# Column sums of exp(phi): four fp32 adds on GpSimd and two fp32 matmuls in place of eighteen bf16 matmuls

## Chip, cores and metric

One core of one Trainium2 chip. The metric is the device time of one execution in microseconds (us). The kernel before takes 271.17 us (median of three runs, 270.51 to 271.28). Engines are named as in the profile: PE is TensorE, PEld its weight loads, DVE VectorE, ACT ScalarE, POOL GpSimd, SP SyncE. "L207" is line 207 of the kernel in question; the changed kernel's lines are shifted by up to twelve.

## The reference

Attention through 32 memory slots, then a two-layer network with a residual, for 8 batches of 8 heads, 576 positions and head size 64:

```python
a = np.exp(phi - np.max(phi, axis=2, keepdims=True))
a = a / (np.sum(a, axis=2, keepdims=True) + 1e-09)     # sum over the 576 positions
k_m = np.einsum('bhsm,bhsd->bhmd', a, k)
v_m = np.einsum('bhsm,bhsd->bhmd', a, v)
scores = scale * np.matmul(q, k_m.transpose(0, 1, 3, 2))
# ... softmax over the 32 slots, times v_m, heads side by side: x (8, 576, 512)
xn = (x - mu) / np.sqrt(var + 1e-06) * g_ln
out = x + np.maximum(xn @ w_ch1, 0.0) @ w_ch2
```

The change concerns only the sum over positions in the second line.

## The kernel before

The maximum is left out. A position is (partition, slot): 64 partitions by nine slots for each half of the heads. The sum over positions is a matmul with a column of one constant (`ones8`, which holds 8.0 and is called a column of ones below), for each slot and half, accumulated in PSUM: eighteen small matmuls in each batch, behind the 72 that make k_m and v_m.

```python
def a_exp(b):
    phi_st, kv, q_bf = loaded[b]
    e = att.tile([P, NS, 4, M], BF16, name="e_sb")
    nc.scalar.activation(out=e..., in_=phi_st..., func=AF.Exp)          # L195

def a_kv(b):
    kv_ps = big([P, 2, 512], FP32, "kv_ps")
    # ... 72 matmuls with e as weights and k|v as moving data: L207
    for c in range(NS):
        for g in range(2):
            r = TS * g
            nc.tensor.matmul(kv_ps[:, g, P:P + 1],                       # L214
                             e[r:r + TS, c].rearrange("p j m -> p (j m)"), ones8[r:r + TS, :],
                             start=(c == 0), stop=(c == NS - 1), tile_position=(r, 0))
    # ... k2 (ACT; in batch 0 DVE) and v2 (DVE) copied out of kv_ps
    nc.vector.reciprocal(out=rs, in_=kv_ps[:, :, P])
```

`a_tr` then transposes k2 and v2 on PE, `a_sc` computes the scores; its exponential uses `rs`. In the steady loop, batch b+1 is prepared between groups of eight matmuls of the second product of batch b:

```python
for b in range(1, B):
    mm1(b, 0, JC)                       # first product, 64 matmuls
    # after group 0 of the second product: a_exp(b+1), a_qT(b+1), a_kv(b+1)
    # after group 1: a_tr(b+1), x_tiles(...)
    # ... a_w1b, a_sc, a_den; at the end load(b+2)
```

Pool issues the loads of k, v and q and, in the start-up, casts three quarters of the second weight to bf16. A copy of one element holds the loads of that weight back until a part of the first has arrived:

```python
def w2_load(n, queue):
    st = wst.tile([P, 4, C], FP32, name="w2_st", bufs=3)
    if n == 0:
        nc.gpsimd.tensor_copy(out=st[0:1, 0, 0:1], in_=w1r[0:1, 3, 1024:1025])   # L143
    queue.dma_start(out=st, in_=w2_v[:, 4 * n:4 * (n + 1), :])
def w2_cast(n):
    nc.gpsimd.tensor_copy(out=w2b[:, 4 * n:4 * (n + 1), :], in_=w2_st[n])        # L148
# ...
w2_load(0, nc.sync)
w2_load(2, nc.sync)
# ...
warm(24)            # matmuls on constants
a_exp(0)
```

## Time and profile before

| | before |
|---|---|
| median time | 271.17 us |
| span of the profiled run | 270.6 us |
| PE busy | 243.6 us, 90% |
| POOL busy | 29.7 us, 11% |
| first transposes (batch 0) | 17.91 us |
| first transposes of batch 1 | 51.32 us |
| matmuls of k and v start, batches 2 to 7 | 76.71, 107.63, 134.30, 165.22, 191.89, 222.82 us |

A line of the timeline gives start, duration, engine, line, operation, output and inputs, sizes and a count; brackets tell how long the engine had been idle before it and what ended that. The granted clock is TensorE's clock in a stretch, as a share of full speed. From 76.71 us on the kernel repeats itself (30.92 and 26.67 us in turn).

### The profile page before, as it was taken

The numbers are of one execution on the slowest core, as the hardware profiler recorded it, in microseconds if no ns is written. First come the engines' busy times: TensorE is split into PE (matmuls) and PEld (weight loads), VectorE is DVE, ScalarE is ACT, GpSimd is POOL, SyncE is SP. The second block draws the span as 40 slices with busy tenths as digits, with TensorE's granted clock in tenths as the row PEclk, the third lists the DMA queues.
The fourth block names the chain that finished last, engine by engine and source line by source line (L and its number), as shares of the span: only waits on it lengthen the run. The fifth ranks groups of instructions, "written<-read, shape, count | busy, mean of one in ns | idle before, by whom it ended". The sixth has DMA issues, their size and how long they took to land.

```text
span 270.6 us, 5662 instructions
## 1 busy us (share of the span) xinstructions
PE 243.6 (90%) x2392; PEld 136.2 (50%) x2423; DVE 153.6 (57%) x302; ACT 128.1 (47%) x218; POOL 29.7 (11%) x47
## 2 busy tenths in 40 slices
PE   6487995985999999999999999999999999999992
PEld 4343562332754366446644475447543665466440
DVE  2227562448638664678375943886386646784431
ACT  3156654051754547255727174448545372555210
POOL 8210053700030000300030003000000000000000
PEclk9968999899999999999999999999999999999998
DMA  6999999999949449792889184965422491121133
GB/s 192 228 207 208 317 311 219 182 208 224 274 76 219 109 86 197 119 221 64 202 135 209 40 209 73 218 147 129 99 49 45 90 198 41 41 55 24 42 76 78
DMA packets 45058, 39.63 MB, mean 146 GB/s; under 512 B 19940, under 2 KB 38376, under 8 KB 45032
## 3 DMA queue, kind: packets, MB, share of 16 engines
q0 software_dynamic: 14784, 16.19, 36.2%
q1 hardware_dynamic: 29192, 21.44, 33.6%
q10 hardware_dynamic: 1056, 1.64, 1.6%
q8 instruction: 19, 0.31, 0.5%
q14 instruction: 7, 0.06, 0.1%
HBM read 41.42 MB, written 9.44 MB: 188 GB/s over the span
## 4 chain that ended last, share of the span: by engine, by line
PE 72%; DMA 12%; DVE 7%; ACT 5%; issue 2%; POOL 0%; DVEq 0%; POOLq 0%
PE ch_ps L396 40%; PE h_ps L338 20%; DMA phi_st<-in_phi_dram 7%; DMA kv_bf<-in_v_dram 5%; PE o_ps L366 3%; PE kv_ps L207 3%; DVE Eh L302 2%; PE w1b_ps L317 2%; ACT rden L299 2%; DVE w1b L321 1%; DVE bst L374 1%; PE sc_ps L280 1%; ACT rden L301 1%; ACT x_sb L370 1%; DVE x_sb L400 1%
## 5 line engine op out<-in xcount | busy, mean ns | idle before, releaser
L396 PE MATMUL ch_ps<-w2b,rT 128*128 128x512 bf16 x547 | 129.5, 382 | 6.2 <-DVE x_sb L400 3.1
L396 PEld LDWEIGHTS <-rT 128*128 128x128 bf16 x576 | 54.4, 98 | 66.3 <-issue 11.4
L338 PE MATMUL h_ps<-Eh,w1b 128*128 128x288 bf16 x512 | 66.7, 285 | 2.8 <-DVE Eh L302 1.6
L344 ACT ACTIVATE rT<-h_ps 128x576 bf16<-128x576 f32 x88 | 52.2, 649 | 29.9 <-PE h_ps L338 29.9
L338 PEld LDWEIGHTS <-w1b 128*128 128x128 bf16 x512 | 49.6, 97 | 19.7 <-issue 4.6
L346 DVE TENSOR_SCALAR rT<-h_ps 128x576 bf16<-128x576 f32 x40 | 30.3, 756 | 27.1 <-PE h_ps L338 27.1
L321 DVE SCALAR_TENSOR_TENSOR w1b<-m_sb,rsum,w1b_ps 128x512 bf16<-128x512 f32 x64 | 43.6, 739 | 2.4 <-ACT m_sb L181 2.0
L370 ACT ACTIVATE x_sb<-o_ps 128x1024 f32<-128x1024 f32 (+1 forms) x20 | 18.8, 938 | 38.9 <-PE o_ps L366 38.9
L400 DVE SCALAR_TENSOR_TENSOR x_sb<-ch_ps,rstd,x_sb 128x512 f32<-128x512 f32 x36 | 26.7, 743 | 16.1 <-PE ch_ps L396 16.1
L374 DVE BATCH_NORM_STATS2 bst<-x_sb 128x6 f32<-128x512 f32 x36 | 24.4, 678 | 13.3 <-ACT x_sb L370 13.3
L302 DVE SCALAR_TENSOR_TENSOR Eh<-E_sb,rs,rden 128x576 bf16<-128x576 bf16 x16 | 12.4, 814 | 17.1 <-ACT rden L301 17.1
L285 ACT ACTIVATE E_sb<-sc_ps,rs 128x640 bf16<-128x640 f32 x16 | 11.9, 791 | 15.7 <-PE sc_ps L280 15.6
L83 POOL DMA_DIRECT2D kv_bf<-in_k_dram x8 | 6.2, 771 | 107.4 <-PE kv_ps L214 106.3
L382 ACT ACTIVATE rstd<-mv,eps_sb 128x2 f32<-128x2 f32 (+1 forms) x20 | 5.9, 295 | 17.0 <-DVE mv L375 17.0
L366 PE MATMUL o_ps<-vb,Eh 128*128 128x256 bf16 (+1 forms) x80 | 12.0, 276 | 1.0 <-DVE Eh L302 1.0
L195 ACT ACTIVATE e_sb<-phi_st 128x1152 bf16<-128x1152 f32 x8 | 9.2, 1151 | 7.4 <-DMA phi_st<-in_phi_dram 7.4
L317 PE MATMUL w1b_ps<-w1r,kvT 64*32 64x512 bf16 x256 | 11.4, 390 | 1.1 <-DVE kvT L238 0.6
L299 ACT ACTIVATE rden<-den_ps 128x576 f32<-128x576 f32 x16 | 9.5, 644 | 5.0 <-PE den_ps L297 5.0
L186 PE MATMUL w_ps<-vmask,blk 128*128 128x256 bf16 x58 | 8.7, 313 | 2.4 <-DVE vmask L130 2.4
L225 DVE CAST v<-kv_ps 128x128 bf16<-128x128 f32 x8 | 2.3, 286 | 15.1 <-ACT k L223 15.1
L207 PE MATMUL kv_ps<-kv_bf,e_sb 64*32 64x128 bf16 x576 | 6.8, 232 | 4.0 <-ACT e_sb L195 3.0
L301 ACT ACTIVATE rden<-rden 128x576 f32<-128x576 f32 x16 | 10.0, 683 | 0.0
(58 smaller groups left out, 116.5 us busy)
## 6 DMA issues: line engine op xcount, KB each, us to landing
out_dram<-x_sb SPq DMA_DIRECT2D x72, 128.0 KB, 2.4
kv_bf<-in_k_dram POOLq DMA_DIRECT2D x8, 576.0 KB, 6.6
kv_bf<-in_v_dram POOLq DMA_DIRECT2D x8, 576.0 KB, 9.7
phi_st<-in_phi_dram SPq DMA_DIRECT2D x7, 576.0 KB, 4.6
q_bf<-in_q_dram POOLq DMA_DIRECT2D x7, 576.0 KB, 12.0
w1r<-in_moe_w_ch_dram POOLq DMA_DIRECT2D x4, 512.0 KB, 17.4
w_st<-in_moe_w_ch_dram SPq DMA_DIRECT2D x2, 1024.0 KB, 16.3
q_st<-in_q_dram SPq DMA_DIRECT2D x1, 1152.0 KB, 11.1
```

The source lines that it names most:

```text
L207: nc.tensor.matmul(kv_ps[32 * j:32 * (j + 1), g, 0:P], e[r:r + TS, c, j, :], kv[r:r + TS, j, :, D * c:D * (c + 1)], start=(c == 0), stop=( ...
L302: nc.vector.scalar_tensor_tensor(out=Eh[:, g, :], in0=s["E"][:, g, 0:S], scalar=s["rs"][:, g:g + 1], in1=rd[:, g].rearrange("p a x -> p (a ...
L317: nc.tensor.matmul(ps[32 * j:32 * (j + 1), g, :], s["kvT"][r:r + 64, 2, 32 * j:32 * (j + 1)], w1r[r:r + 64, j, fs], start=True, stop=True, ...
L321: nc.vector.scalar_tensor_tensor(out=s["w1b"][:, g, fs], in0=m_sb[:, fs], scalar=s["rsum"][:, g:g + 1], in1=ps[:, g, :], op0=ALU.mult, op1 ...
L338: nc.tensor.matmul(h_ps[:, half, 0:HS], s["w1b"][:, g, P * j:P * (j + 1)], s["Eh"][:, g, HS * half:HS * (half + 1)], start=(g == 0), stop= ...
L344: nc.scalar.activation(out=dst, in_=h_ps[:, :, 0:HS], func=AF.Relu)
L346: nc.vector.tensor_scalar(out=dst, in0=h_ps[:, :, 0:HS], scalar1=0.0, scalar2=None, op0=ALU.max)
L366: nc.tensor.matmul(ov[:, :, g, :], s["Eh"][:, g, a:z], s["vb"][:, g].rearrange("p j d -> p (j d)"), start=True, stop=True)
L370: nc.scalar.activation(out=x[:, 0:n], in_=o_ps[:, 0:n], func=AF.Copy)
L374: nc.vector.bn_stats(out=stt, in_=x[:, i, :])
L396: nc.tensor.matmul(ch_ps, rT[:, j, P * t:P * (t + 1)], w2b[:, j, :], start=(j == 0), stop=(j == JC - 1))
L400: nc.vector.scalar_tensor_tensor(out=x, in0=ch_ps, scalar=rstd, in1=x, op0=ALU.mult, op1=ALU.add)
```

## The change

The intent is to take work off PE, the busiest engine, and give it to Pool, the idlest: Pool adds the nine slots in fp32 (slots 0 to 3 to slots 4 to 7, then two of the four results to the other two, then one to one, then the ninth slot), and PE sums over partitions with one fp32 matmul for each half. These two stand ahead of the transposes.

```diff
-    ones8 = consts.tile([P, 1], BF16, name="ones8")
+    ones8 = consts.tile([P, 1], FP32, name="ones8")
@@ a_exp
+        es = att.tile([P, P], FP32, name="es")
+        ev = e.rearrange("p c j m -> p c (j m)")
+        nc.gpsimd.tensor_tensor(out=a4, in0=ev[:, 0:4], in1=ev[:, 4:8], op=ALU.add)     # L200
+        nc.gpsimd.tensor_tensor(out=a2, in0=a4[:, 0:2], in1=a4[:, 2:4], op=ALU.add)     # L202
+        nc.gpsimd.tensor_tensor(out=es, in0=a2[:, 0], in1=a2[:, 1], op=ALU.add)         # L203
+        nc.gpsimd.tensor_tensor(out=es, in0=es, in1=ev[:, 8], op=ALU.add)               # L204
@@ a_kv
-        for c in range(NS):
-            for g in range(2):
-                ... the eighteen matmuls, L214 above
@@ new
+    def a_sum(b):
+        for g in range(2):
+            r = TS * g
+            nc.tensor.matmul(kv_ps[:, g, P:P + 1], s["es"][r:r + TS, :], ones8[r:r + TS, :],
+                             start=True, stop=True, tile_position=(r, 0))               # L235
+        nc.vector.reciprocal(out=rs, in_=kv_ps[:, :, P])
@@ a_tr
+        a_sum(b)
         t_ps = big([P, 3, P], BF16, "kvT_ps")
```

## The prediction

> **What bounds the kernel now.** I read the page first: engine shares and the chain that ended last.
>
> ```profile
> span 270.6 us, 5662 instructions
> ## 1 busy us (share of the span) xinstructions
> PE 243.6 (90%) x2392; PEld 136.2 (50%) x2423; DVE 153.6 (57%) x302; ACT 128.1 (47%) x218; POOL 29.7 (11%) x47
> ...
> PE 72%; DMA 12%; DVE 7%; ACT 5%; issue 2%; POOL 0%; DVEq 0%; POOLq 0%
> ```
>
> TensorE (PE) is the bound on average, and Pool looks free. But the chain is 12% DMA, so the kernel has two stages. I split the span with the table by stretch (columns: length, busy time of PE, PEld, DVE, ACT and POOL, granted clock, DMA share, GB/s):
>
> ```profile
> 13.65:17.90 4.25, 3.30 (x112) 2.46 (x112) 0.47 (x2) 2.70 (x3) 1.14 (x2) 0.70 1.24 207
> 17.90:21.35 3.45, 3.23 (x33) 1.05 (x33) 0.91 (x5) 1.48 (x2) 0.00 (x0) 0.50 1.24 206
> ...
> 42.30:45.27 2.97, 0.01 (x1) 0.00 (x0) 0.00 (x0) 1.21 (x2) 1.38 (x1) 1.00 1.13 207
> 45.27:51.50 6.23, 6.01 (x108) 3.10 (x109) 1.89 (x6) 2.13 (x6) 4.53 (x8) 0.73 1.23 164
> ...
> 165.20:191.90 26.70, 26.25 (x283) 14.82 (x287) 17.73 (x34) 14.69 (x25) 2.48 (x4) 1.00 0.76 155
> 191.90:222.80 30.90, 29.95 (x295) 16.71 (x299) 19.45 (x37) 15.67 (x28) 0.00 (x0) 1.00 0.42 84
> ```
>
> From 76.7 us on, one batch takes 26.7 or 30.9 us and PE is busy for 97 to 98% of it: what PE executes or waits for there is paid for in full. The first 45 us are different: PE has holes, one of 2.97 us at 42.30 because phi of batch 1 lands late. The clock was low around 18 us and again after that hole (0.73).
>
> The concerned stretch of a steady batch, from the timeline (start, duration, engine, line, operation; batch 6 is prepared here):
>
> ```profile
> 190.69 1.15 ACT L195 ACTIVATE e_sb<-phi_st 128x1152 bf16<-128x1152 f32 x1
> 191.89 0.80 PE L207 MATMUL kv_ps<-kv_bf,e_sb 64*32 64x128 bf16 x72
> 192.63 0.38 PE L214 MATMUL kv_ps<-ones,e_sb 64*128 64x1 bf16 x18
> 193.16 1.67 PE L396 MATMUL ch_ps<-w2b,rT 128*128 128x512 bf16 x7 [0.16 <-issue]
> 194.67 0.27 PE L234 MATMUL kvT_ps<-ident,k 128*128 128x128 bf16 x2
> ```
>
> The eighteen sum matmuls hold PE from 192.69 to 193.00, 0.31 us in the chain of waits (0.31 to 0.33 in every batch): 17 ns each, though each record says 160 ns, because they are pipelined. Then come eight matmuls of the second product and the transposes at 194.67, that is 2.83 us after the exponential ended (191.84).
>
> **What the Trainium skill says.** "GPSIMD Engine Reference", section 3.1: a two-input fp32 add takes about 2.6 cycles per element, 4497 ns for 2048 elements. The trace has no Pool add; its one-input casts of 2048 elements take 1895 ns, a copy of one element 0.18 us. "FP8 and Floating Point Precision", TensorE Precision Notes: true fp32 takes four passes through the array. "TensorE: Matmul & The Clock Gate", weight-path section: the fast weight load is not used for fp32, and loading takes the columns over 1.2 (128 columns: 107 ns). The trace has no fp32 matmul, so it neither confirms nor denies these two. The same page, Part 1: after an idle window of about 3.4 us the clock halves, and it returns after a busy window. The trace agrees: PE idles 3.67 us before 13.65, and the granted clock is then 0.70 and 0.50.
>
> **The change part by part, steady batches.** (a) Removed: eighteen matmuls, 0.31 us of PE per batch. (b) Added on PE: two fp32 matmuls with 128 columns of weights each. My estimate from the skill: four loads of 107 ns make 0.43 us for one matmul; the two use different row halves and may overlap in part, or not at all: 0.25 to 0.9, taken as 0.5 us. So the replacement of eighteen by two saves nothing. (c) Added on Pool: adds of 512, 256, 128 and 128 elements, in series, 1024 in all. At 4497/2048 = 2.2 ns an element that is 2.25 us, plus a start and a handover for each of four dependent instructions; with the 0.1 to 0.2 us that small Pool instructions take here, 2.6 to 3.2 us (estimate). (d) Moved: the sums now stand just ahead of the transposes in PE's order, and PE takes instructions in order. Without the eighteen, PE gets there at 194.67 - 0.31 = 194.36, which is 2.5 us after the exponential. The Pool sums are ready 2.6 to 3.2 us after it, plus 0.1 to 0.2 for the two semaphores: PE waits 0.2 to 0.9, I take 0.5. Sum per batch: -0.31 + 0.5 + 0.5 = +0.7 us. Six batches (2 to 7) are prepared in the steady stage: 6 x 0.7 = +4.2 us. The reciprocal moves behind the sums but its user, the score exponential at 199.89, is 5 us away; it costs nothing.
>
> **The prologue.** This is the larger term. The built order of Pool shows where the adds of batch 0 fall: not right after the exponential (done at 5.9 us) but after the one-element copy of line 143, which holds back the loads of the second weight until a piece of the first one has landed. Pool's timeline, PE's timeline and the chain of waits of the kernel before:
>
> ```profile
> 23.50 0.17 POOL L143 CAST w_st<-w1r 1x1 f32<-1x1 bf16 x1 [6.62 <-DMA w1r<-in_moe_w_ch_dram]
> ...
> 17.91 0.39 PE L234 MATMUL kvT_ps<-ident,k 128*128 128x128 bf16 x2
> ...
> 38.70 3.61 PE L396 MATMUL ch_ps<-w2b,rT 128*128 128x512 bf16 x15
> 45.27 0.80 PE L207 MATMUL kv_ps<-kv_bf,e_sb 64*32 64x128 bf16 x72 [2.96 <-ACT e_sb L195]
> ...
> 24.19 19.85 DMA phi_st<-in_phi_dram
> ```
>
> Pool cannot begin the adds of batch 0 before 23.7; they end at 26.3 to 26.9. PE, which went to the transposes at 17.91, now waits some 9 us for the sums, and with two cold fp32 matmuls reaches them at about 27.1: **9.2 us late**. All of the first batch (scores, exponentials, the first product) follows from there, in order, up to the end of the first quarter of the second product (42.3 before). PE is cold after this wait, as it was before, but some 1.5 us more of the work falls into the cold time: +0.6. So that quarter ends near 42.3 + 9.2 + 0.6 = 52.1. Before, PE then waited until 45.27 for phi of batch 1. That load is issued by ScalarE after the logarithms of batch 0, so it too goes 9.2 us later (33.4); but the same bytes are in flight before and after at over 200 GB/s, and all of them had landed by 47.2 before, so I expect it by 48, while ScalarE gets to this exponential at about 48.6. So the hole of 2.97 us goes. The low clock after it goes too: the next sixteen matmuls took 5.07 us (46.41 to 51.48) and should take some 3.6 at full clock. The transposes of batch 1 are then at 52.1 + 0.8 + 3.6 + 0.4 = 56.9 against 51.5: **+5.4 us** remain of the 9.2, and nothing later has slack to take them up.
>
> Sum: 271.2 + 5.4 + 4.2 = 280.8; I say 280.5.
>
> **Loads.** Pool also issues the k, v and q loads. Before, those of batch b+2 are issued as soon as the matmuls of batch b free the buffer (77.83, 108.75 in the trace); now they stand behind the adds of batch b+1, a whole batch later (near 110 for the one of 77.83). They are needed one batch (27 to 31 us) after that and take 6.6 to 12 us to land: no wait.
>
> **The rivals.** R1, no wait in steady batches: Pool adds at the one-input rate (0.93 ns an element) would end 1.5 us after the exponential, and with cheap fp32 matmuls (0.25 us) the steady batches change by nothing: 276.5. For it: the skill's add figure is for fp32 inputs, half of these are bf16. Against it: two operands share one read port there. R2, Pool much slower (mixed types, dependent handovers; 4.5 us for the chain): a wait of 2 us per batch, 6 x 2.2 = 13 and the prologue +7: 291. R3, the prologue wait is hidden, because the stage is bound by transfers: then +1 to +4 in all, 272 to 275. Against it: only 2.97 us of hole plus the clock loss stand between the prologue's PE chain and its end, less than 9. R4, what the change intends: eighteen matmuls of 160 ns each off PE, 8 x 2.9 = 23 us saved. Against it: the chain shows 0.31 us, not 2.9; even with free sums the most is 8 x 0.31 = 2.5 us, under 1%.
>
> **Range and chances.** The prologue term is 4 to 8, the steady term -1 to +9; both positive in most draws: 276 to 287 holds it 8 times in 10. Faster by 2% would need all of R3 and more: 0.01. Within 2% (below 276.6): R1 or R3, 0.13. Slower: 0.86.
>
> **What would show it right or wrong.** In the profile of the changed kernel: a PE hole of 8 to 9 us from about 18 to 26.5, ended by Pool's last add, with the copy of line 143 just before the adds; no hole before the matmuls of batch 1, which start near 52; Pool's four adds about 1.2, 0.65, 0.35 and 0.35 us apart; six PE waits of 0.2 to 0.9 us on Pool; two fp32 matmuls costing 0.25 to 0.9 us before the transposes; batches of 27.4 and 31.6 us; no wait for k, v or q loads. I am wrong if the adds of batch 0 run early, if phi of batch 1 lands after 50, or if the Pool chain differs from 2.6 to 3.2 us.

## The result, and the profile after

The changed kernel takes **284.5 us** (median of four runs, 284.3 to 285.44), against 271.23 us (median of four runs, the three above and one more) before. The ratio is 1.0497, with a 95% interval of 1.0462 to 1.0532: slower by 5%. Ratios here are the mean time of one kernel's fast runs over that of the other's of the same rounds, so not quite the ratio of the medians.

The shares of the chain that ended last, by engine, of the kernel after:

```profile
PE 62%; ACT 11%; DVE 9%; POOL 8%; DMA 6%; issue 2%; POOLq 0%; DVEq 0%
```

Pool was 0% of this chain and is now 8%. One steady batch of the kernel after, from the timeline:

```profile
174.20 1.15 ACT L195 ACTIVATE e_sb<-phi_st 128x1152 bf16<-128x1152 f32 x1
175.40 0.80 PE L215 MATMUL kv_ps<-kv_bf,e_sb 64*32 64x128 bf16 x72
175.43 1.15 POOL L200 TENSOR_TENSOR es<-e_sb 128x512 f32<-128x512 bf16 x1 [25.94 <-ACT e_sb L195]
176.65 0.72 POOL L202 TENSOR_TENSOR es<-es 128x256 f32<-128x256 f32 x1
177.45 0.45 POOL L203 TENSOR_TENSOR es<-es 128x128 f32<-128x128 f32 x1
177.98 0.42 POOL L204 TENSOR_TENSOR es<-es,e_sb 128x128 f32<-128x128 f32 x1
178.46 0.39 PE L235 MATMUL kv_ps<-ones,es 64*128 64x1 f32 x4 [0.43 <-POOL es L204]
178.78 0.29 PE L246 MATMUL kvT_ps<-ident,k 128*128 128x128 bf16 x2
```

From the first matmul of k and v to the transposes it was 194.67 - 191.89 = 2.78 us, and is 178.78 - 175.40 = 3.38. The difference of 0.60 is paid in each steady batch: the starts of these matmuls are now 85.05, 116.58, 143.86, 175.40, 202.67 and 234.20, so five batches take 149.15 us in place of 146.11.

The start-up of the kernel after, Pool and PE, from the timeline:

```profile
22.99 0.17 POOL L143 CAST w_st<-w1r 1x1 f32<-1x1 bf16 x1 [6.64 <-DMA w1r<-in_moe_w_ch_dram]
23.14 1.14 POOL L200 TENSOR_TENSOR es<-e_sb 128x512 f32<-128x512 bf16 x1
...
26.17 0.59 PE L235 MATMUL kv_ps<-ones,es 64*128 64x1 f32 x4 [9.09 <-POOL es L204]
26.69 0.39 PE L246 MATMUL kvT_ps<-ident,k 128*128 128x128 bf16 x2
...
55.05 0.80 PE L215 MATMUL kv_ps<-kv_bf,e_sb 64*32 64x128 bf16 x72
```

PE waits 9.09 us for the adds of batch 0, whose input had been ready since 5.8 us. The wait for phi of batch 1 that stood in this place before (2.96 us, ahead of the matmuls at 45.27) is gone: at 55.05 no wait is shown. But the whole start-up is later than I had predicted (55.05 and not 52.1), and between the transposes and those matmuls stands something that the prediction does not have. DVE, Pool and PE in the same stretch:

```profile
32.88 3.18 DVE L314 SCALAR_TENSOR_TENSOR Eh<-E_sb,rs,rden 128x576 bf16<-128x576 bf16 x2 [0.50 <-ACT rden L313]
33.03 2.41 POOL L148 CAST w2b<-w_st 128x2048 bf16<-128x2048 f32 x1 [6.92 <-DMA w_st<-in_moe_w_ch_dram]
37.25 1.86 PE L350 MATMUL h_ps<-Eh,w1b 128*128 128x288 bf16 x8 [0.25 <-ACT rT L356]
...
44.35 3.73 POOL L148 CAST w2b<-w_st 128x2048 bf16<-128x2048 f32 x2 [8.91 <-DMA w_st<-in_moe_w_ch_dram]
...
46.54 1.88 DVE L262 TENSOR_TENSOR vb<-v,vmask 128x256 bf16<-128x256 bf16 x2
```

The same instructions of DVE in the kernel before (there L302 and L250), and its first two casts:

```profile
24.22 1.55 DVE L302 SCALAR_TENSOR_TENSOR Eh<-E_sb,rs,rden 128x576 bf16<-128x576 bf16 x2 [0.62 <-ACT rden L301]
34.69 0.49 DVE L250 TENSOR_TENSOR vb<-v,vmask 128x256 bf16<-128x256 bf16 x2
36.76 3.73 POOL L148 CAST w2b<-w_st 128x2048 bf16<-128x2048 f32 x2 [13.08 <-DMA w_st<-in_moe_w_ch_dram]
```

The two instructions of L314 take 3.18 us after the change; before, the same two took 1.55 us (24.22 to 25.77). The two of L262 take 1.88 us against 0.49. In both places a weight cast of Pool runs at the same time. Before, the casts ran at 36.76 to 40.49 and 43.89 to 45.79, when both of these pairs of DVE were over (at 25.77 and 35.18). The casts wait for transfers and do not move with the computation (the first now comes 3.7 us earlier, the last 2.3 us later), while the computation moved 9 us towards them.

The balance of the two profiled runs (282.6 - 270.6 = 12.0 us): the transposes of batch 1 start at 59.66 in place of 51.32, **+8.34**; from there to the matmuls of batch 2 both take 25.39 us, 0; five steady batches, **+3.04**; the rest, in which the last batch is prepared, 48.40 against 47.78, **+0.62**. (The profiled run of the kernel before, 272.34 us, is 1.1 us above the median; so the profiles differ by 12.0 us and the medians by 13.3.)

### The profile page after: what moved, and what is told of

It is laid out like the page before. It is cut to its first block, busy times and chain, and to the rows that moved or that the text cites. A ratio compares the mean times of both kernels' runs of the same rounds, so it can differ in the third digit from the quotient of the medians.

```text
span 282.6 us, 5519 instructions
## 1 busy us (share of the span) xinstructions
PE 249.5 (88%) x2311; PEld 136.6 (48%) x2311; DVE 158.2 (56%) x302; ACT 127.7 (45%) x218; POOL 52.6 (19%) x79
## 4 chain that ended last, share of the span: by engine, by line
PE 62%; ACT 11%; DVE 9%; POOL 8%; DMA 6%; issue 2%; POOLq 0%; DVEq 0%
PE ch_ps L408 32%; PE h_ps L350 19%; DMA w1r<-in_moe_w_ch_dram 6%; DVE Eh L314 3%; PE o_ps L378 3%; ACT rT L356 3%; POOL es L200 3%; ACT e_sb L195 2%; PE w1b_ps L329 2%; ACT rden L311 2%; DVE w1b L333 2%; POOL es L202 2%; PE m_ps L172 2%; DVE bst L386 1%; PE sc_ps L292 1%
## 5 line engine op out<-in xcount | busy, mean ns | idle before, releaser
L408 PE MATMUL ch_ps<-w2b,rT 128*128 128x512 bf16 x576 | 134.1, 380 | 3.1 <-DVE x_sb L412 3.1
L350 PE MATMUL h_ps<-Eh,w1b 128*128 128x288 bf16 x512 | 67.5, 287 | 5.3 <-DVE Eh L314 3.2
L358 DVE TENSOR_SCALAR rT<-h_ps 128x576 bf16<-128x576 f32 x40 | 30.1, 755 | 27.6 <-PE h_ps L350 27.6
L200 POOL TENSOR_TENSOR es<-e_sb 128x512 f32<-128x512 bf16 x8 | 9.2, 1147 | 152.2 <-ACT e_sb L195 152.2
L314 DVE SCALAR_TENSOR_TENSOR Eh<-E_sb,rs,rden 128x576 bf16<-128x576 bf16 x16 | 14.0, 916 | 17.0 <-ACT rden L313 17.0
L235 PE MATMUL kv_ps<-ones,es 64*128 64x1 f32 x32 | 3.3, 270 | 11.7 <-POOL es L204 11.7
L378 PE MATMUL o_ps<-vb,Eh 128*128 128x256 bf16 (+1 forms) x80 | 12.1, 276 | 1.0 <-DVE Eh L314 1.0
L186 PE MATMUL w_ps<-vmask,blk 128*128 128x256 bf16 x58 | 9.6, 334 | 2.4 <-DVE vmask L130 2.4
L235 PEld LDWEIGHTS kv_ps<-ones,es 64*128 64x128 f32 x32 | 2.6, 200 | 15.5 <-POOL es L204 15.1
```

The lines of the kernel that those rows point to most:

```text
L200: nc.gpsimd.tensor_tensor(out=a4, in0=ev[:, 0:4], in1=ev[:, 4:8], op=ALU.add)
L314: nc.vector.scalar_tensor_tensor(out=Eh[:, g, :], in0=s["E"][:, g, 0:S], scalar=s["rs"][:, g:g + 1], in1=rd[:, g].rearrange("p a x -> p (a ...
L350: nc.tensor.matmul(h_ps[:, half, 0:HS], s["w1b"][:, g, P * j:P * (j + 1)], s["Eh"][:, g, HS * half:HS * (half + 1)], start=(g == 0), stop= ...
L358: nc.vector.tensor_scalar(out=dst, in0=h_ps[:, :, 0:HS], scalar1=0.0, scalar2=None, op0=ALU.max)
L378: nc.tensor.matmul(ov[:, :, g, :], s["Eh"][:, g, a:z], s["vb"][:, g].rearrange("p j d -> p (j d)"), start=True, stop=True)
L408: nc.tensor.matmul(ch_ps, rT[:, j, P * t:P * (t + 1)], w2b[:, j, :], start=(j == 0), stop=(j == JC - 1))
```

## The experiments

My theory: (1) most of the start-up's loss is the order of Pool's instructions, with the adds behind the copy that waits for a weight; (2) a part of it is Pool's casts meeting DVE's instructions of two SBUF inputs; (3) the steady loss is a wait for the Pool chain and the cost of fp32 matmuls, each about half. The rivals: the start-up is bound by transfers whatever the order; the wait in the steady batches is not Pool's; the later loads of k, v and q cost something; the eighteen matmuls were worth what their records say.

| kernel | median us (runs) | ratio to before, 95% interval | five steady batches, us | wait on Pool in a steady batch |
|---|---|---|---|---|
| before | 271.24 (13) | 1 | 146.11 | none |
| changed | 284.5 (4) | 1.0497 (1.0462 to 1.0532) | 149.15 | 0.43 |
| e1_early | 276.42 (6) | 1.0181 (1.0138 to 1.0224) | 149.25 | 0.44 |
| e2_early_late | 273.79 (6) | 1.0111 (1.0074 to 1.0147) | 146.72 | none on PE |
| e3_early_bf16 | 275.50 (6) | 1.0087 (1.0018 to 1.0155) | 148.33 | 0.44 |
| e4_early_late_bf16 | 270.98 (6) | 1.0000 (0.9962 to 1.0039) | 145.63 | none on PE |
| e5_gate | 281.79 (6) | 1.0417 (1.0381 to 1.0454) | 149.16 | 0.43 |
| e6_double | 273.77 (6) | 1.0109 (1.0062 to 1.0155) | 147.21 | no Pool adds |
| e7_loads_ahead | 285.77 (6) | 1.0555 (1.0523 to 1.0587) | 149.17 | 0.43 |
| e8_early_cast | 277.62 (6) | 1.0236 (1.0193 to 1.0279) | 149.24 | 0.44 |
| e9_all | 270.10 (6) | 0.9945 (0.9898 to 0.9991) | 145.66 | none on PE |

All nine gave correct results. The 13 runs of the kernel before are those of the experiments' rounds; the changed kernel was run with the four above. "Five steady batches" is from the first matmul of k and v of batch 2 to that of batch 7, in the profiled run. Medians are over all runs, ratios over the fast ones: one run of the kernel before, one of e1, four of e3 (its profiled run too) and one of e9 were counted as slow. e3's median is thus mostly of slow runs; its two fast ones took 271.42 and 275.01. A slow run by that count is one that is 1.5% above the fastest of its kernel, and on one core it cannot be told from the spread between runs.

### e1: the adds of batch 0 earlier in Pool's order

```diff
     kv1 = load_kv(1)
+    a_exp(0)                 # with its adds; its definition moves up
     q1 = load_q(1)
@@
     warm(24)
-    a_exp(0)
```

> Changed kernel, with the adds of batch 0 placed in Pool's order right after the loads of k and v of batch 1 (Pool idles there from 8.4 to 12.8 us and the exponential is done at 5.9), ahead of the copy that waits for the first weight. Theory (the prologue loss is Pool's order): the PE hole of 9.1 us before the first sums goes, and with it the low clock and the Pool casts that met VectorE's two-input instructions; what remains is the steady loss of 0.61 us for six batches: 271.2 + 3.7 = 274.9, so 274.2 to 275.8. Rival (the prologue is bound by transfers, or by something that the order does not set): 281 to 285.

Measured: 276.42 us, 8.1 us less than the changed kernel. PE's hole before the first sums went from 9.09 to 0.50 us, and it is DVE, not Pool, that ends it. The exponential of batch 0 stays where it was (4.74 us, before 4.72). Part (1) stands, and "bound by transfers" falls as the reason for the loss: the same bytes are moved. It does not fall for what is left: in e1's profile, too, PE waits in the start-up for what a transfer holds back (2.53 us at 37.23 for a weight cast). The first two sum groups of e1 on PE:

```profile
15.13 0.39 PE L236 MATMUL kv_ps<-ones,es 64*128 64x1 f32 x4 [0.50 <-DVE v L228]
46.77 0.39 PE L236 MATMUL kv_ps<-ones,es 64*128 64x1 f32 x4 [1.57 <-POOL es L132]
```

The time is 1.5 us above what I expected (274.9), though the steady batches are as expected. The second line offered a reason, tested in e8.

### e2: e1 with the sums later on PE

```diff
     def a_tr(b):
-        a_sum(b)
@@ x_tiles(pr, ts, mid=None), behind its matmuls
+        if mid is not None:
+            mid()
@@ steady loop; batches 0 and 1 call a_sum right behind a_tr
-        ex[1] += [lambda: x_tiles(pr, t1)]
+        ex[1] += [lambda: x_tiles(pr, t1, (lambda: a_sum(nb)) if nb < B else None)]
```

> As e1, with the two fp32 sum matmuls behind the transposes and the four matmuls of the next product tile (some 0.5 us later on PE), where the Pool chain of 3.05 us is done. Theory (a wait of 0.43 us per steady batch on Pool's last add): it goes, 6 x 0.43 = 2.6 less than e1: 272.3 (271.8 to 273.0), so still not below the kernel before. Rival (the wait shown is only the time in which PE loads fp32 weights, or VectorE's later reciprocal holds the buffer back): no gain on e1, or less than 1 us.

Measured: 2.53 us less than e1 over five batches, 0.51 us for each, and 2.6 us less in the median. PE no longer waits:

```profile
194.71 0.28 PE L246 MATMUL kvT_ps<-ident,k 128*128 128x128 bf16 x2
194.83 0.43 POOL L132 TENSOR_TENSOR es<-es,e_sb 128x128 f32<-128x128 f32 x1
195.40 0.39 PE L236 MATMUL kv_ps<-ones,es 64*128 64x1 f32 x4
```

The transposes now run 0.12 us before Pool's last add begins, and the sums follow without a gap on PE. So the wait was Pool's, and cost half a microsecond per batch. The level, 273.79, is above the expected range, as e1's was. Still, e2's steady batches take 0.12 us more each than those of the kernel before: the sums remain dearer than the eighteen matmuls. Over six batches that is 0.7 us of the 1.1% (3 us) by which e2 is above. The two profiled runs differ by about as much (271.2 and 270.6 us); where the rest lies is not shown.

### e3: e1 with the sums in bf16

```diff
-    ones8 = consts.tile([P, 1], FP32, name="ones8")
+    ones8 = consts.tile([P, 1], BF16, name="ones8")
-        nc.gpsimd.tensor_tensor(out=es, in0=a2[:, 0], in1=a2[:, 1], op=ALU.add)
-        nc.gpsimd.tensor_tensor(out=es, in0=es, in1=ev[:, 8], op=ALU.add)
+        nc.gpsimd.tensor_tensor(out=a1, in0=a2[:, 0], in1=a2[:, 1], op=ALU.add)   # fp32
+        nc.gpsimd.tensor_tensor(out=es, in0=a1, in1=ev[:, 8], op=ALU.add)         # es in bf16
```

> As e1, with the last add written as bf16 and the column of ones in bf16, so the two sum matmuls are one pass each; place of the sums as in the change. Theory (the two fp32 matmuls cost 0.32 us per batch on PE): 6 x 0.29 = 1.7 less than e1: 273.2 (272.6 to 273.8). Rival (fp32 loads hide beside other matmuls): within 0.5 of e1.

Measured: over five batches 0.92 us less than e1, 0.18 us for each. From the sums to the transposes it is now 0.10 us instead of 0.32, while the wait stays:

```profile
170.34 0.18 PE L237 MATMUL kv_ps<-ones,es 64*128 64x1 bf16 x2 [0.44 <-POOL es L133]
170.44 0.28 PE L248 MATMUL kvT_ps<-ident,k 128*128 128x128 bf16 x2
```

So fp32 costs about 0.2 us per batch more than bf16, less than the 0.29 that I expected here. The median, 275.50, is outside the expected range; the times of e1 and e3 are too spread to say anything on 1 us, and the steady batches decide.

### e4: all three mended

The diffs of e1, e2 and e3 together.

> All three mended: early adds, late sums, bf16 sums. Theory (the eighteen matmuls cost at most 0.31 us per batch): 271.2 - 6 x 0.28 = 269.5 (269.0 to 270.8), that is 0.2 to 0.8% below the kernel before. Rival (the eighteen matmuls cost what their records say, 160 ns each, 2.9 us per batch): 250 to 256.

Measured: 270.98 us, ratio 1.0000. The steady batches take 145.63 us in place of 146.11: 0.10 us less for each, not the 0.28 that I expected. With every new cost but two bf16 matmuls taken away, nearly nothing is left to win, and the rival of 250 to 256 us is out. The trace shows where the expected 0.28 went: the two bf16 sum matmuls still move what follows by 0.2 us. The transposes start 2.47 us after the matmuls of k and v (before: 2.78, so the 0.31 do appear), and the group behind them starts 0.81 us after the transposes in place of 0.61. Free sums could thus have won about 0.3 us per batch at most.

### e5: Pool's casts kept away from DVE's two-input instructions

```diff
     for n in range(3):
+        if n == 0:
+            nc.gpsimd.tensor_copy(out=w2b[0:1, 0, 0:1], in_=st8[0]["Eh"][0:1, 1, S - 1:S])
+        if n == 1:
+            nc.gpsimd.tensor_copy(out=w2b[0:1, 4, 0:1], in_=st8[0]["vb"][0:1, 1, 3, D - 1:D])
         w2_cast(n)
```

This is the changed kernel with two copies of one element, which make the casts wait for DVE's results and are overwritten by them.

> Changed kernel, with two one-element Pool copies that hold Pool's weight casts back until VectorE has written the scaled exponentials and the masked v of batch 0. Nothing else moves. Theory (the Pool casts at 33.0 and 44.3 us shared the SBUF port with VectorE's instructions of two SBUF inputs: 3.18 us for the two of the one kind in place of 1.55, and 1.88 for the two of the other in place of 0.49): both groups go back to 1.55 and 0.49 us, the waits of 1.95 and 0.88 us on PE shrink to about 0.3 and 0, and the time falls by 1.5 to 3.0 us to 281.5 to 283. If the long gap also set the clock drop at 37 us, up to 1 us more. Rival (VectorE was slow there for another reason): the durations stay at 3.18 and 1.88 and the time at 284 to 285.

Measured: 281.79 us, 2.7 us less than the changed kernel. From the timeline of e5:

```profile
33.25 1.55 DVE L314 SCALAR_TENSOR_TENSOR Eh<-E_sb,rs,rden 128x576 bf16<-128x576 bf16 x2 [0.73 <-ACT rden L313]
36.00 1.19 PE L350 MATMUL h_ps<-Eh,w1b 128*128 128x288 bf16 x8 [0.25 <-ACT rT L356]
43.72 0.48 DVE L262 TENSOR_TENSOR vb<-v,vmask 128x256 bf16<-128x256 bf16 x2
51.20 0.80 PE L215 MATMUL kv_ps<-kv_bf,e_sb 64*32 64x128 bf16 x72
```

Both groups of DVE are back at 1.55 and 0.48 us, and the eight matmuls that took 1.86 us after the longer gap take 1.19: the clock no longer drops there (from 37.25 to 40.80 the granted clock is 0.54 in the changed kernel and 1.00 in e5). The matmuls of batch 1 start at 51.20, and the transposes of batch 1 at 55.80. Part (2) stands. The Trainium skill has this, "SBUF — State Buffer", section "Who interferes with whom": a DVE instruction with two SBUF inputs contends with a GpSimd instruction that reads SBUF, because its second input comes through the shared read interface, and the second to issue blocks. The runs agree: one of the two L314 instructions took 2.44 us, and the cast beside it 2.41 in place of 1.90; one of the two L262 took 1.68 in place of 0.28, and the casts beside it were not longer (3.73 for two).

### e6: the eighteen matmuls twice

```diff
+        for c in range(NS):
+            for g in range(2):
+                r = TS * g
+                nc.tensor.matmul(kv_ps[:, g, P + 1:P + 2], ... as L214, into a column that nobody reads
```

> Kernel before, with the eighteen sum matmuls of every batch issued twice (the second set to a column that nobody reads). Theory (they run at 17 ns each, pipelined): 0.31 us per batch, 7 batches on the path: +2.2, 273.4 (272.3 to 274.0). Rival (160 ns each, as their records say): +2.9 us per batch, 291 to 295.

Measured: over five batches 1.10 us more than before, 0.22 us for each set of eighteen, or 12 ns a matmul. The records say 160 ns each:

```profile
193.56 0.80 PE L207 MATMUL kv_ps<-kv_bf,e_sb 64*32 64x128 bf16 x72
194.30 0.38 PE L214 MATMUL kv_ps<-ones,e_sb 64*128 64x1 bf16 x18
194.54 0.36 PE L220 MATMUL kv_ps<-ones,e_sb 64*128 64x1 bf16 x18
196.57 0.28 PE L240 MATMUL kvT_ps<-ident,k 128*128 128x128 bf16 x2
```

The second eighteen start 0.24 us after the first: this is the price, and not the 2.9 us that 18 x 160 ns would make.

### e7: the loads of k, v and q a batch earlier

```diff
+            if nb + 1 < B:
+                ex[0] += [lambda: load_ahead(nb + 1)]      # k, v and q, ahead of the adds of a_exp(nb)
             ex[0] += [lambda: a_exp(nb), ...]
-                ex[7] += [lambda: load(nb + 1)]
+                ex[7] += [lambda: load_rest(nb + 1)]       # phi
```

> Changed kernel, with the loads of k, v and q of batch b+2 ahead of the adds of batch b+1 in Pool's order, so that they are issued a batch earlier, as in the kernel before. Theory (the later loads cost nothing): 284.5 within 0.7, batches unchanged at 27.3 and 31.5 us. Rival (part of the loss is transfers that now run beside the stores and the loads of phi): 1 to 3 us less.

Measured: 285.77 us, and 149.17 us for five batches, as in the changed kernel (149.15). So the later loads cost nothing in the steady batches, and the rival's gain does not come. The median is 1.3 us above the changed kernel's, outside the expected 0.7; why is not shown.

### e8 and e9: the third cast behind the adds of batch 1

```diff
-    for n in range(3):
+    for n in range(2):
         w2_cast(n)
@@
     a_exp(1)
+    w2_cast(2)
```

> As e1, with the third weight cast of Pool behind the adds of batch 1 in place of ahead of them. Theory (in e1 the adds of batch 1 stood behind a cast that waits for a transfer, and PE waited 1.57 us for them in the profiled run): that wait goes, 0.5 to 1.6 less than e1, so 274.8 to 275.9. Rival (the 1.5 us by which e1 was above its expectation is spread of the start-up alone): same as e1, 276.4 within 0.6.

Measured: 277.62 us, no gain on e1's 276.42; it lies above both ranges. The theory fails as a reason for e1's 1.5 us. In the profiled run of e8 phi of batch 1 arrived late enough that Pool idled 4.92 us before these adds; the wait of 1.57 us in e1's profile belongs to a run in which phi came earlier.

> As e4, with the third weight cast behind the adds of batch 1 as in e8. In e4 no wait for them showed. Theory: the five steady batches take 0.10 us less each than in the kernel before (as in e4: 145.6 in place of 146.1), so 270.3 (269.3 to 271.3) and not to be told from the kernel before. Rival: a gain of 1% or more, if the start-up had been e4's limit.

Measured: 270.10 us, ratio 0.9945 (0.9898 to 0.9991), five batches 145.66 us. Of all that I ran this is the fastest. Its interval ends just below 1, so the gain over the kernel before is half a per cent if it is one, and far from the 1% of the rival; that of the steady batches alone is 6 x 0.09 = 0.5 us or 0.2%.

What is left of e1's and e8's distance from 274.9 most likely lies in the start-up, since the steady batches and the end agree in their profiles. From the transposes of batch 1 to the matmuls of batch 2, the profiled runs take 25.39 us (before, changed, e6, e7), 26.3 (e3, e5, e8) or 27.4 to 27.6 (e1, e2, e4, e9), with the same work but for the sums. In all of them PE idles 3.11 us in the middle, for DVE's last step of a tile. The stretch after it, from the table by stretch, of the kernel before and then of e1 (length, busy times of PE, PEld, DVE, ACT and POOL, granted clock, DMA share, GB/s):

```profile
64.60:76.71 12.11, 11.77 (x82) 7.54 (x82) 7.27 (x12) 8.86 (x15) 0.00 (x0) 1.00 1.05 239
```

```profile
60.40:74.66 14.26, 14.23 (x83) 8.55 (x83) 7.45 (x12) 9.13 (x15) 0.00 (x0) 0.79 0.64 147
```

The clock fell to 0.79 in e1 and not in the kernel before, at the same idle time. The other profiles go the same way: in this stretch the clock is 1.00 where it takes 12.1 us (before, changed, e6, e7), 0.87 where it takes 13.0 (e3, e5, e8) and 0.79 to 0.80 where it takes 14.1 to 14.3 (e1, e2, e4, e9). So within the profiles the clock accounts for the 1 to 2 us. Why it falls in some, I have not shown: there is only one profile of each kernel. For the timed runs the record has the mean granted clock: it goes with the time in e1 (0.986 at 274.08 us, 0.967 at 278.86), in e6 and in e9 (0.992 at 266.88, 0.974 at 271.91), but not in the kernel before (0.986 at 271.64, 0.973 at 270.27). So the clock is a likely part of the spread between runs, not all of it. Nor does this stretch explain e1's 1.5 us: e1's profiled run is its fastest, 274.08.

## Why the prediction was right

It said 280.5 us and a range of 276 to 287, slower with a chance of 0.86. Measured: 284.5. It forecast +9.3 us and the medians differ by 13.3; the mechanism was right, and one term, the start-up, was mis-sized. By its steps:

- **Steady batches.** Predicted +0.7 us each, found +0.61. The Pool chain was put at 2.6 to 3.2 us and took 3.05 (175.35, the end of the exponential, to 178.40). The wait was put at 0.5: PE's gap shows 0.43, and e2 takes off 0.51. The gap understates it, since it counts from the modelled end of the matmul before: the sums start 3.06 us after the matmuls of k and v (175.40 to 178.46), where PE is ready after 2.47 (e2 and e4), so they come 0.59 late. The removed matmuls were put at 0.31: e4 shows that the transposes come 0.31 earlier, e6 that one set is worth 0.22. The fp32 matmuls were put at 0.5 and took 0.32: mis-sized. So the sum is -0.31 + 0.59 + 0.32 = 0.60; that the predicted 0.7 is near it owes something to two errors of opposite sign.
- **The hole at 18 us.** Predicted 8 to 9 us, ended by Pool's last add; found 9.09 and so ended. The transposes were put 9.2 us late and are 8.78 late (26.69 against 17.91). Pool's order in the built program gave this away; the diff does not tell it, since `a_exp` is called in a place where ACT is free, while Pool's order has the waiting copy first. e1 shows that it is the cause.
- **The hole of 2.97 us goes.** Right: no wait at 55.05, and the sixteen matmuls behind take 3.56 us, as put (3.6). Phi of batch 1 landed at 47.2, where the prediction has "by 48".
- **The start-up term, +5.4, was too small.** Found +8.34. The step that failed is "All of the first batch (scores, exponentials, the first product) follows from there, in order", which moves the computation as a rigid block. It moved into Pool's weight casts, which follow the transfers; DVE lost 1.63 and 1.39 us to them, and the clock dropped once more. PE's delay against the kernel before shows it: 8.66 us at the first product (33.75 against 25.09), 10.29 behind the first collision (36.11), 11.86 behind the clock drop (41.15), 12.87 behind the second collision (50.61 against 37.74). The +0.6 for a longer cold time did not come in its place: from these transposes to the denominators it is 3.93 us in both kernels. e5, without the collisions, has the matmuls of batch 1 at 51.20 and the transposes at 55.80, where the prediction has 52.1 and 56.9: without them the prediction would have been 1 us too late here.
- **The loads.** Predicted free; e7 agrees.
- **The rivals.** R1 needed a faster Pool and R2 a slower one; the chain took what was put (R1's cheap fp32 matmuls, 0.25 us, were near the 0.32 found). R3, a hidden wait with +1 to +4 us in all, is refuted by the 13.3 us and by e1. R4 is refuted by e4 and e6.

## What to carry to other kernels

Value a group of small matmuls by the spacing of their starts, not by their records: eighteen of 160 ns each were worth 0.2 to 0.3 us. When work goes to an engine that looks idle, read that engine's order of instructions, for a wait that stands there for another purpose is inherited by everything behind it; and a consumer on the busiest engine should stand at least the whole chain's length behind the producer. A delay in a start-up full of transfers does not move everything together: what waits for transfers does not move with it, and instructions that share a port can then meet.

## What the Trainium skill lacked or had wrong

- "GPSIMD Engine Reference", section 3.1, has the fp32 add at 2048 elements alone (4497 ns, 2.2 ns an element). Here adds of 128 and 256 fp32 elements took 453 and 722 ns, which is 2.1 ns an element and some 180 ns fixed (worked out from the two), with 0.08 us between dependent adds. The page has no figure for bf16 inputs: 512 of them into fp32 took 1147 ns.
- "FP8 and Floating Point Precision", TensorE Precision Notes, speaks of four passes for fp32. The trace shows two weight loads and two matmuls for each fp32 matmul, and the two fp32 matmuls together hold PE for 0.32 us, against 0.10 for two in bf16. From "TensorE: Matmul & The Clock Gate" I had worked out 0.43 us for one. (The prediction names its weight-path section for this; the loading time, the columns over 1.2, stands in the section before it, "LDWEIGHTS (loading the stationary operand)".)
- "TensorE: Matmul & The Clock Gate", Part 1, puts the idle time before the clock halves at about 3.4 us or more (a table near the end of the page says gaps over about 3). Here 3.11 us without a matmul (by their recorded ends) were followed by a granted clock of 1.00 in four profiles and of 0.79 to 0.87 in seven. And in the changed kernel the clock was 0.54 from 37.25 to 40.80 behind gaps of 1.25 and 1.95 us, with two matmuls between them.
- "SBUF — State Buffer", section "Who interferes with whom", agrees with e5; it gives two factors of slowing (6.8 for DVE, 1.5 for GpSimd) and no duration. One 128x576 instruction of DVE took 2.44 us beside a cast of 2048 elements on Pool, in place of 0.82.
